# The diagonal term of a chunked attention from narrow products, and a shorter router, in a fused attention, router and MLP kernel

## The chip, the cores and the metric

The kernel runs on one core of one Trainium2 chip. Its time is the device time in microseconds (us) of one execution. Five engines work beside each other, each through its own queue of instructions: TensorE (PE, its weight loads PEld), VectorE (DVE), ScalarE (ACT), GpSimd (POOL) and SyncE (SP), which here only issues transfers. An instruction waits at the head of its engine's queue until what it reads is there and what it overwrites is free.

## The reference

Three parts follow each other: a linear attention with a state that decays per channel, a mixture of 8 experts with one expert per token, and a gated MLP.

```python
# attention: B, H, S, D = 4, 8, 768, 48
for t in range(S):
    cur = np.einsum('bhd,bhe->bhde', u[None] * kt, vt)
    y[:, :, t] = np.einsum('bhd,bhde->bhe', rt, state + cur)
    state = wt[:, :, :, None] * state + np.einsum('bhd,bhe->bhde', kt, vt)
# experts: N, D, E, F = 3072, 384, 8, 1024
logits = xn @ en.T / tau                  # x and expert_emb divided by (norm + 1e-6)
expert_idx = np.argmax(logits, axis=1)
probs = np.exp(logits - logits.max(-1, keepdims=True))
probs /= probs.sum(-1, keepdims=True) + 1e-09
out[mask] = gate_w[mask, None] * (np.maximum(x[mask] @ w1[e], 0.0) @ w2[e])
# second MLP: 384 -> 2048 -> 384
g = h * np.tanh(log1p(exp(h)))            # h = x @ w_in
return g @ w_out
```

The term `cur` is the bonus: for one token it adds (sum over d of r·u·k) times v. In a chunk of tokens it stands on the diagonal of the matrix of products of r and k.

## The kernel before

**Attention** (`attention`). The 768 tokens are cut into 12 chunks (NCH) of C = 64. Each chunk s holds 16 blocks (NB: 4 batches times 4 pairs of heads); on the 128 partitions lie the channels of two heads, 64 rows each (48 used). Per chunk, in `scaled`: ScalarE squares `w` for a check of its range (L513), VectorE scans `w` forwards (`pre`, L516), takes a reciprocal (L518) and scans backwards (`suf`, L520); GpSimd multiplies r by `pre` into `rh` and VectorE k by `suf` into `kh`, both in two halves of 128x512 (L525). In `scores`: ScalarE scales r by u into `ur` (4 instructions, L548); TensorE forms the dots of `kh` and `rh` (64 products of 64x64, L543) and, by the same helper `dots`, those of k and `ur`. The attention matrix `at` of a chunk has a half per head of the pair. For head 0 VectorE copies the dots under the mask `after` (strictly later tokens, L554); for head 1 ScalarE copies all of them (L556), and GpSimd clears what is not later by two selects (L558). Then VectorE copies, for both heads, the diagonal of the products of k and `ur` under the mask `same` (L563). In `carried`: TensorE transposes `kh` (L575), ScalarE copies that (L578), TensorE forms the sums for the state (L587), VectorE, or VectorE and GpSimd, the new state (L597, L600 and L602). In `outputs`: TensorE multiplies `rh` with the state (L616) and `at` with v (L621), and ScalarE copies the result to `x` (L631).

**Loads.** SyncE loads w, r, k and v of the chunks; each has two or three buffers (NW, NR, NK, NV = 3, 2, 3, 3; r and k as loaded have NR = 2), so a load waits for the last reader of the buffer's last contents. All loads stand in one queue (L487).

**Router** (`Router`). Every chunk gives two tiles of 128 tokens. `tile`: TensorE transposes the tile (L324), ScalarE copies it (L332) and sums its squares (L333), TensorE forms the logits (six half products, L329), ScalarE copies them (L335). `decide` runs over groups of tiles, ROUTED = [6, 6, 4, 4, 2, 2]: 20 small VectorE operations per group find the expert, its gate and the row (`inv_norm` L274 to L279, L356 to L360, ranks L378 to L382, gate L384 to L388), with matmuls for the running count (L369 to L373). `send` (L394) scatters each tile's rows to its experts' slots by a GpSimd transfer `xs`.

**Behind it** come short warming matmuls (L972), the experts (`experts`) and the second MLP (`moe2`). They start when the last send has been issued.

**The order.** All of attention and router is a list of steps, each with its engine, an estimated cost, what it reads and what it writes. `Plan.order` is a list scheduler: by the costs, the wake times and due times (`late`) it chooses the next step, and so fixes every engine's queue and which of the seven PSUM banks a step gets. A step is one or several instructions; `at`, `ur`, `kh` and so on name the tiles that the profile prints.

Of the kernel before, what the change touches and what calls it, by code (L numbers as in the profile page):

```python
# [43 lines left out]
ROUTED = [6, 6, 4, 4, 2, 2]  # L44
# [10 lines left out]
STEP, APART = 0.12, 0.0  # L55
FAR, LEAST = 45.0, 1e-10
LN_EXP = 6

# [10 lines left out]
class Plan:  # L69
# [13 lines left out]
    def add(self, eng, us, fn, reads=(), writes=(), wake=None, late=0.0, port=None, apart=0.0):  # L83
        o = SimpleNamespace(eng=eng, us=us, fn=fn, wake=self.WAKE[eng] if wake is None else wake, need=set(),
                            late=late, apart=apart, port=eng == "pool" if port is None else port, n=len(self.steps), ps=[k for k in {*reads, *writes} if k[0] == "ps"])
# [49 lines left out]
    def wait(self, o, q):  # L135

        return 0.0 if o.eng == q.eng and o.eng in ("pe", "sp") else o.wake

    def order(self):
        S = self.steps  # L140
        way = [0.0] * len(S)
        out = [[] for _ in S]
        for o in S:
            for p in o.need:
                out[p].append(o.n)
        for o in reversed(S):
            way[o.n] = o.us + max([self.wait(o, S[q]) + way[q] for q in out[o.n]] + [o.late])
        waits = [len(o.need) for o in S]
        ready = {o.n: 0.0 for o in S if not o.need}
        at, done = {}, {}  # L150
        banks = [(0.0, b) for b in self.g.banks]
        left = {k: len(u) for k, u in self.users.items()}
        seen = {}
        while ready:
            can = []
            for n, t in ready.items():
                o = S[n]
                t = max(t, at.get(o.eng, 0.0), at.get("port", 0.0) if o.port else 0.0, at.get("apart", 0.0) if o.apart else 0.0)
                new = sum(k not in self.bank for k in o.ps)
                if new:  # L160
                    if len(banks) < new:
                        continue
                    t = max(t, sorted(x[0] for x in banks)[new - 1])
                can.append((t, n))
            t0, n0 = min(can)
            eng = S[n0].eng
            first = lambda cs: min(cs, key=lambda c: (-way[c[1]], c[1]))
            t, n = first([c for c in can if S[c[1]].eng == eng and c[0] <= t0 + SLACK])
            if S[n].port:
                t, n = first([c for c in can if S[c[1]].port and c[0] <= t + SLACK])  # L170
                eng = S[n].eng
            o = S[n]
            for k in o.ps:
                if k not in self.bank:
                    banks.sort(key=lambda x: x[0])
                    self.bank[k] = banks.pop(0)[1]
            o.fn()
            del ready[n]
            at[eng] = t + o.us
            if o.port:  # L180
                at["port"] = t + o.us
            if o.apart:
                at["apart"] = t + o.apart
            done[n] = t + o.us
            for k in o.ps:
                left[k] -= 1
                seen[k] = max(seen.get(k, 0.0), t + o.us + o.wake)
                if not left[k]:
                    banks.append((seen[k], self.bank[k]))
            for q in out[n]:  # L190
                waits[q] -= 1
                if not waits[q]:
                    ready[q] = max(done[p] + self.wait(S[p], S[q]) for p in S[q].need)
        assert len(done) == len(S)


def dve(n):
    return 0.07 + n / 960


def act(n):
    return 0.06 + n / 1150
# [6 lines left out]
def setup(g, tmp, plan, then):  # L209
# [9 lines left out]
    g.oh, g.dest, g.desti = t("oh", [128, NT, E], BF16), t("dest", [128, NT]), t("desti", [128, NT], I32)  # L219
# [26 lines left out]
def setup_experts(g, tmp, plan, then):  # L246
# [9 lines left out]
    rn = inv_norm(g, plan, ss, *[tmp.tile([E, 1], F32, name=f"nrme{i}") for i in range(4)], "e", "e_ss", "e_rn")  # L256
# [9 lines left out]
def inv_norm(g, plan, ss, r, t, r2, out, nm, src, dst):  # L266
# [31 lines left out]
class Router:  # L298


    def __init__(self, g, pool, plan, sizes, xs):
# [7 lines left out]
            ("ss", [128, G]), ("lg", [128, G, E]), ("ca", [128, G, E]), ("nr", [128, G]), ("rn", [128, G]), ("sm", [128, G]))}) for i in range(2)]  # L309
        self.group = [(q, sum(sizes[:q]), n) for q, n in enumerate(sizes) for _ in range(n)]  # L310

    def tile(self, j):
# [18 lines left out]
        add("pe", 0.4, turn, [kx, "ident"], [k])  # L331
        add("act", 0.42, lambda: nc.scalar.copy(xT, plan.view(k, KC, 128)), [k], [kT])  # L332
        add("act", 0.7, lambda: nc.scalar.activation(self.sq, x[:, :DM], AF.Square, accum_out=q.ss[:, i:i + 1]), [kx], [("ss", par, i)])  # L333
        add("pe", 0.4, logits, [kT, "enT"], [k])
        add("act", 0.2, lambda: nc.scalar.copy(q.lg[:, i], lg()), [k], [("lg", par, i)])  # L335
# [3 lines left out]
    def decide(self, qi, j0, G):  # L339
# [3 lines left out]
        ss, sm, gt = q.ss[:, :G], q.sm[:, :G], self.xs[:, j0 % NX:j0 % NX + G, DM]  # L343
        at = iter(range(SMALL + 72 * par, 512, 6))
        mx, mn, nt, r2 = [g.bank[:, c:c + G] for c, _ in zip(at, range(4))]
        d = g.bank[:, SMALL + 72 * par + 24:][:, :G * E].rearrange("p (t e) -> p t e", e=E)
        one = lambda x: x.rearrange("p (t o) -> p t o", o=1).to_broadcast(full)
        lg, ca = q.lg[:, :G], q.ca[:, :G]
# [15 lines left out]
        rn = inv_norm(g, self.plan, ss, q.nr[:, :G], nt, r2, q.rn[:, :G], f"x{par}", ("ssall", par), kn)  # L364
# [3 lines left out]
        def rank():  # L368
            nc.tensor.matmul(rt()[:, :G].rearrange("p t e -> p (t e)"), lhsT=g.tri, rhs=oh.rearrange("p t e -> p (t e)"), start=True, stop=False)  # L369
            nc.tensor.matmul(rt()[:, G], lhsT=g.ones, rhs=oh[:, 0], start=False, stop=G == 1)  # L370
# [979 lines left out]
```

## Time and profile before

| | |
|---|---|
| runs of the kernel | 837.56 us (median of 832.56, 837.56, 838.58) |
| the execution profiled | 838.25 us; its span, from first to last instruction, 836.4 us |
| busy in the span | PE 770.5, DVE 651.7, ACT 487.5, POOL 401.9 us |
| TensorE's granted clock, mean | 0.960 |
| last send of the router issued | 187.24 us |
| attention and router, 0 to 187.24 us | PE 138.72, DVE 138.68, ACT 95.73, POOL 89.19 us busy |
| experts and second MLP, 199.00 to 836.40 us | PE 621.59 of 637.40 us busy |

The granted clock is a share of full speed. In a row of a view grouped by lines, the busy time is followed by the mean length of one instruction in ns and by the idle time of the engine just before these instructions, with what ended it. A mean can be longer than busy time divided by count, since instructions of one engine overlap.

### The profile page before, as it was taken

What the parts mean: (1) busy time and instruction counts of PE and PEld (TensorE: products, weight loads), DVE (VectorE), ACT (ScalarE), POOL (GpSimd) and SP (SyncE); (2) the same over time, 40 slices, a digit from 0 to 9 for tenths busy, and PEclk for the clock granted to TensorE, in tenths of its full rate; (3) what the DMA queues carried; (4) which work ended last, traced back from release to release, by engine and by line L of the source; (5) the groups of instructions that cost most, each with busy time, mean ns of one, the idle gap of its engine ahead of it and who ended that gap; (6) DMA issues with size and microseconds to landing.
All of it is one profiled execution on the core that took longest, in us unless ns stands there. A gap on an engine that the chain in (4) does not pass through costs nothing. (4 is left out here: it accounts for less than half of the span.)

```text
span 836.4 us, 18791 instructions
## 1 busy us (share of the span) xinstructions
PE 770.5 (92%) x7152; PEld 704.1 (84%) x7152; DVE 651.7 (78%) x999; ACT 487.5 (58%) x1000; POOL 401.9 (48%) x378
## 2 busy tenths in 40 slices
PE   2887788968999999999999999999999999999995
PEld 2776676747999999889989999999999999999995
DVE  9888867447889888998978887786876886877783
ACT  4664554424665566457556666656656656655653
POOL 7354454335677787776623344334334334334331
PEclk9898879869999999999999999999999999999998
DMA  6665445117777767767500000001001001001001
GB/s 166 175 183 165 148 140 160 54 74 185 185 201 200 181 188 196 192 153 215 127 1 1 1 10 29 1 1 39 1 0 38 1 1 38 0 1 38 1 1 42
DMA packets 61362, 73.87 MB, mean 88 GB/s; under 512 B 8966, under 2 KB 51886, under 8 KB 61262
## 3 DMA queue, kind: packets, MB, share of 16 engines
q1 hardware_dynamic: 57422, 63.11, 27.9%
q0 software_dynamic: 3840, 9.47, 3.1%
q8 instruction: 58, 0.95, 0.5%
q14 instruction: 42, 0.34, 0.1%
HBM read 61.86 MB, written 10.69 MB: 87 GB/s over the span
## 5 line engine op out<-in xcount | busy, mean ns | idle before, releaser
L1142 POOL TENSOR_TENSOR t<-t,t 128x512 f32<-128x512 f32 x94 | 122.0, 1299 | 237.2 <-ACT t L1138 234.4
L1151 DVE TENSOR_TENSOR gl<-t,gh 128x512 fp32r<-128x512 f32 (+1 forms) x97 | 114.1, 1176 | 74.5 <-ACT gh L1148 74.2
L1135 ACT ACTIVATE t<-t,two 128x512 f32<-128x512 f32 (+1 forms) x97 | 69.9, 720 | 118.4 <-DVE t L1132 118.4
L863 PE MATMUL acc<-woh,gl 128*128 128x384 f32 x384 | 129.6, 338 | 0.1
L861 PE MATMUL acc<-woh,gh 128*128 128x384 f32 x384 | 129.3, 337 | 0.0
L862 PE MATMUL acc<-wol,gh 128*128 128x384 f32 x384 | 129.0, 336 | 0.0
L940 POOL TENSOR_TENSOR w0l<-r,w0h 128x384 fp32r<-128x384 f32 x63 | 68.3, 1084 | 59.4 <-ACT w0h L939 53.1
L856 PE MATMUL ph<-xl,wih 128*128 128x512 f32 x240 | 95.0, 396 | 0.0
L855 PE MATMUL ph<-xh,wil 128*128 128x512 f32 x240 | 94.8, 395 | 0.0
L854 PE MATMUL ph<-xh,wih 128*128 128x512 f32 x240 | 93.3, 389 | 0.0
L861 PEld LDWEIGHTS acc<-woh,gh 128*128 128x128 f32 x384 | 72.2, 188 | 4.2
L862 PEld LDWEIGHTS acc<-wol,gh 128*128 128x128 f32 x384 | 72.1, 188 | 4.0
L940 POOL TENSOR_TENSOR w1l<-r,w1h 128x384 fp32r<-128x384 f32 x63 | 74.5, 1183 | 2.0 <-ACT w1h L939 1.5
L863 PEld LDWEIGHTS acc<-woh,gl 128*128 128x128 f32 x384 | 72.0, 188 | 0.4 <-DVE gl L1151 0.4
L856 PE MATMUL acc<-hl,w1h 128*128 128x428 f32 (+7 forms) x192 | 67.3, 350 | 3.8 <-DVE hl L1021 3.6
L1145 DVE TENSOR_TENSOR t<-t,ph 128x512 f32<-128x512 f32 (+1 forms) x97 | 64.8, 668 | 5.8 <-POOL t L1142 5.7
L854 PE MATMUL acc<-hh,w1h 128*128 128x428 f32 (+7 forms) x192 | 67.6, 352 | 1.8 <-DVE yT L1036 1.8
L1148 ACT CAST gh<-t 128x512 fp32r<-128x512 f32 (+1 forms) x97 | 58.8, 606 | 16.6 <-DVE t L1145 14.2
L1132 DVE SCALAR_TENSOR_TENSOR t<-t 128x512 f32<-128x512 f32 (+1 forms) x97 | 66.2, 683 | 2.1 <-ACT t L1128 2.1
L1125 DVE TENSOR_SCALAR t<-ph 128x512 f32<-128x512 f32 (+1 forms) x97 | 65.3, 674 | 2.1 <-PE ph L856 1.7
L855 PE MATMUL acc<-hh,w1l 128*128 128x428 f32 (+7 forms) x192 | 66.1, 344 | 0.0
L854 PE MATMUL ph<-xh,w0h 128*128 128x420 f32 (+7 forms) x189 | 65.0, 344 | 0.0
(213 smaller groups left out, 1810.6 us busy)
## 6 DMA issues: line engine op xcount, KB each, us to landing
r<-in_moe_w SPq DMA_DIRECT2D x128, 192.0 KB
d<-in_moe_w_in SPq DMA_DIRECT2D x16, 384.0 KB
d<-in_moe_w_out SPq DMA_DIRECT2D x16, 384.0 KB
r<-in_r_t SPq DMA_DIRECT2D x24, 192.0 KB
k<-in_k_t SPq DMA_DIRECT2D x24, 192.0 KB
v<-in_v_t SPq DMA_DIRECT2D x24, 192.0 KB
w<-in_w_t SPq DMA_DIRECT2D x22, 198.0 KB
xs<-zs SPq DMA_DIRECT2D x1, 1203.1 KB
```

What stands on the lines that cost most here:

```text
L854: mm(out, lhsT=wh, rhs=xh, start=start, stop=False)
L855: mm(out, lhsT=wl, rhs=xh, start=False, stop=False)
L856: mm(out, lhsT=wh, rhs=xl, start=False, stop=stop)
L861: mm(out, lhsT=ah, rhs=bh, start=start, stop=False)
L862: mm(out, lhsT=ah, rhs=bl, start=False, stop=False)
L863: mm(out, lhsT=al, rhs=bh, start=False, stop=stop)
L940: (eng or nc.gpsimd).tensor_tensor(lo, r, f32(hi), op=ALU.subtract)
L1125: nc.vector.tensor_scalar(tile_of(i, "t0", mt, bufs=3)[:, q], S[i]["ph"][:, q], 20.0, None, op0=ALU.min)
L1132: nc.vector.scalar_tensor_tensor(t0, t0, 2.0, t0, op0=ALU.add, op1=ALU.mult)
L1135: nc.scalar.activation(tile_of(i, "t1", mt)[:, q], S[i]["t0"][:, q], AF.Ln, bias=g.two)
L1142: (nc.gpsimd if i < TI - 2 else nc.vector).tensor_tensor(t0, t0, S[i]["t1"][:, q], op=ALU.mult)
L1151: nc.vector.tensor_tensor(tile_of(i, "gl", ghl, F32R)[:, q], S[i]["t0"][:, q], f32(S[i]["gh"][:, q]), op=ALU.subtract)
```

## The change

**The bonus.** Per chunk GpSimd multiplies r by k without scaling into one buffer `rk` (two halves, L551 of the new kernel). TensorE multiplies each 128x128 block of it by a narrow matrix `ub` of 2 columns, u of either head (8 products), with two filler products of 128x512 in bf16 ahead of them (FILL), and ScalarE copies the 128x16 results to `bon`. For head 0 ScalarE writes `same` scaled by a column of `bon` into `at` (8 instructions of 128x64), for head 1 GpSimd multiplies `same` by `bon` in one instruction of 128x512 (`ON_POOL`). The dots of `kh` and `rh` come after that, and VectorE copies them into `at` under `after`, for both heads. The scaling `ur`, the products of k and `ur`, ScalarE's copy, the selects and the copies under `same` are gone. The range check looks at `bon` too.

**The router** has five groups, [6, 6, 6, 4, 2]; the normalisation has one operation fewer; the running count is added by a matmul with the identity and kept by a ScalarE copy; 1e-9 stands as a ninth column that the sum takes in; the logits take three whole products.

**The order** is no longer computed. `ORDER` lists all steps in sequence and `BANKS` gives the PSUM banks, so each engine's queue follows the list.

```diff
-ROUTED = [6, 6, 4, 4, 2, 2]
+ROUTED = [6, 6, 6, 4, 2]
+FILL = 2
+ON_POOL = [(s, 1) for s in range(NCH)]
+ORDER = [
+    2, 16, 18, 6, 3, 4, 10, 0, 20, 19, 27, 9, 8, 11, 5, 7, 31, 12, 17, 32, 25, 29, 37, 38,
...
+]
...
     def order(self):
...
+        bank = iter(BANKS)
+        for n in ORDER:
+            o = self.steps[n]
             for k in o.ps:
                 if k not in self.bank:
+                    self.bank[k] = self.g.banks[int(next(bank))]
             o.fn()
...
-            ("dve", lambda: v.scalar_tensor_tensor(t, ss, -0.5, r, op0=ALU.mult, op1=ALU.mult), [src, kr], kt),
-            ("dve", lambda: v.tensor_tensor(t, t, r, op=ALU.mult), [kr], kt),
-            ("dve", lambda: v.scalar_tensor_tensor(r2, t, 1.5, r, op0=ALU.add, op1=ALU.mult), [kr], kt),
-            ("dve", lambda: v.tensor_tensor(t, ss, r2, op=ALU.mult), [src], kt),
-            ("dve", lambda: v.tensor_scalar(t, t, 1e-6, None, op0=ALU.add), [], kt),
+            ("dve", lambda: v.tensor_tensor(t, ss, r, op=ALU.mult), [src, kr], kt),
+            ("dve", lambda: v.tensor_tensor(r, t, r, op=ALU.mult), [kt], kr),
+            ("dve", lambda: v.scalar_tensor_tensor(t, r, -3.0, t, op0=ALU.add, op1=ALU.mult), [kr], kt),
+            ("dve", lambda: v.tensor_scalar(t, t, -0.5, 1e-6, op0=ALU.mult, op1=ALU.add), [], kt),
...
-                for h in COLS:
-                    nc.tensor.matmul(lg()[h], lhsT=xT[:, c, h], rhs=g.enT[:, c], start=c == 0, stop=c == KC - 1)
+                nc.tensor.matmul(lg(), lhsT=xT[:, c], rhs=g.enT[:, c], start=c == 0, stop=c == KC - 1)
...
+            nc.tensor.matmul(rt(), lhsT=g.ident, rhs=g.runs[:, qi:qi + 1].to_broadcast([128, G + 1, E]), start=False, stop=G == 1)
...
-        add("dve", n, lambda: v.tensor_tensor(rk(), rk(), g.runs[:, qi:qi + 1].to_broadcast(full), op=ALU.add), [("runs", qi), kr], [RK])
-        add("dve", n, lambda: v.tensor_tensor(g.runs[:, qi + 1], g.runs[:, qi], rt()[:, G], op=ALU.add), [kr, ("runs", qi)], [("runs", qi + 1)])
...
-        add("dve", n, lambda: v.tensor_scalar(sm, sm, 1e-9, None, op0=ALU.add), [], [SM])
...
-        for j in range(NP):
-            add("act", 0.43, lambda j=j: a.activation(UR[:, B * j:B * j + B], R[nr][:, B * j:B * j + B], AF.Copy, scale=uc[:, j:j + 1]),
-                [("r", nr), "uc"], [("ur", j)])
-        add("pe", 1.08, dots(ks, KH[nk], RH[nk]), hats, ks, late=late(s) + LATE_A)
-        add("dve", 0.63, lambda: v.copy_predicated(at[:, 0], mask(after), plan.view(ks[0], 2 * NP, C)),
-            [ks[0], "masks"], [("at", n, 0)])
-        add("act", act(512), lambda: a.copy(at[:, 1], plan.view(ks[1], 2 * NP, C)), [ks[1]], [("at", n, 1)])
-        for q in range(2):
-            add("pool", 0.65, lambda q=q: p.affine_select(
-                out=at[ROW[q], 1], in_=at[ROW[q], 1], pattern=[[0, 2 * NP], [1, C]], compare_op=ALU.is_ge, fill=0.0,
-                base=-1, channel_multiplier=-1), [], [("at", n, 1)])
-        add("pe", 1.08, dots(kb, K[nr], UR), [("k", nr)] + [("ur", j) for j in range(NP)], kb)
-        for h in range(2):
-            add("dve", 0.63, lambda h=h: v.copy_predicated(at[:, h], mask(same), plan.view(kb[h], 2 * NP, C)),
-                [kb[h], "masks"], [("at", n, h)])
+        def bonus():
+            for _ in range(FILL):
+                pe.matmul(plan.view(kb, 512), lhsT=g.ident.bitcast(BF16)[:, :128], rhs=g.wide, start=True, stop=True)
+            for jp in range(2 * NP):
+                pe.matmul(plan.view(kb, 2 * NP, 2)[:, jp], lhsT=RK[:, 2 * jp:2 * jp + 2].rearrange("p b t -> p (b t)"), rhs=ub[:, jp // 2],
+                          start=True, stop=True)
+
+        def own(h):
+            for jp in range(2 * NP):
+                a.activation(at[:, h, jp], same, AF.Copy, scale=BON[:, s, jp, h:h + 1])
+
+        for i, c in enumerate(halves):
+            add("pool", 1.2, lambda c=c: p.tensor_tensor(RK[:, c], R[nr][:, c], K[nr][:, c], op=ALU.mult),
+                [("r", nr), ("k", nr)], [("bon", i)])
+        add("pe", 0.9 + 0.22 * FILL, bonus, [("bon", 0), ("bon", 1), "ub", "ident", "wide"], [kb], recs=32 + 2 * FILL)
+        add("act", 0.2, lambda: a.copy(BON[:, s], plan.view(kb, 2 * NP, 2)), [kb], [("own b", s)])
+        for h in range(2):
+            if (s, h) in ON_POOL:
+                add("pool", 1.19, lambda h=h: p.tensor_tensor(at[:, h], same.rearrange("p (o t) -> p o t", o=1).to_broadcast([128, 2 * NP, C]),
+                                                              bc(BON[:, s, :, h]), op=ALU.mult), [("own b", s), "masks"], [("at", n, h)])
+            else:
+                add("act", 8 * 0.35, lambda h=h: own(h), [("own b", s), "masks"], [("at", n, h)])
+        add("pe", 1.08, dots, hats, ks, late=late(s) + LATE_A, recs=128)
+        for h in range(2):
+            add("dve", 0.71, lambda h=h: v.copy_predicated(at[:, h], mask, plan.view(ks[h], 2 * NP, C)), [ks[h], "masks"], [("at", n, h)])
```

How the queues move. First VectorE, in the middle of the chunks of the kernel before; the numbers behind the names are buffers (`pre_141`, `pre_142` are used in turn, and `at_117`, `at_118`):

```order
L600 TENSOR_TENSOR sum_126<-bank_80,state_125 128x384
L518 RECIPROCAL w_134<-pre_141 128x16
L563 COPY_PREDICATED at_117<-same_132,bank_83 128x512
L563 COPY_PREDICATED at_117<-same_132,bank_84 128x512
L520 SCALAR_TENSOR_TENSOR suf_143<-w_134,bank_79 128x1056
L554 COPY_PREDICATED at_118<-after_131,bank_81 128x512
L516 SCALAR_TENSOR_TENSOR pre_142<-w_135,bank_79 128x1056
L525 TENSOR_TENSOR kh_112<-k_138,suf_143 128x512 x2
```

And VectorE in the changed kernel, at a like place (L509 and L513 are now the scans, L511 the reciprocal, L518 `kh`, L565 the copy with `after`, L601 the sum):

```order
L518 TENSOR_TENSOR kh_109<-k_139,suf_144 128x512 x2
L509 SCALAR_TENSOR_TENSOR pre_141<-w_134,bank_79 128x1056
L565 COPY_PREDICATED at_115<-after_131,bank_85 128x512
L511 RECIPROCAL w_134<-pre_141 128x16
L565 COPY_PREDICATED at_115<-after_131,bank_80 128x512
L513 SCALAR_TENSOR_TENSOR suf_143<-w_134,bank_79 128x1056
L601 TENSOR_TENSOR sum_124<-bank_85,state_122 128x384
```

Three masked copies stood around the two scans of a chunk; now two stand there, both with `after`. GpSimd in the kernel before, at such a place:

```order
L525 TENSOR_TENSOR rh_115<-r_136,pre_141 128x512 x2
L558 AFFINE_SELECT at_118<-at_118 64x512 x2
L525 TENSOR_TENSOR rh_116<-r_137,pre_142 128x512
L602 TENSOR_TENSOR state_125<-sum_126,own_127 128x384 x2
L525 TENSOR_TENSOR rh_116<-r_137,pre_142 128x512
```

And GpSimd in the changed kernel (`rk` is L551, `rh` L518, the spread of head 1 L558, the state L603):

```order
L518 TENSOR_TENSOR rh_113<-r_136,pre_141 128x512 x2
L558 TENSOR_TENSOR at_115<-same_132,bon_129 128x512
L518 TENSOR_TENSOR rh_114<-r_137,pre_142 128x512
L551 TENSOR_TENSOR rk_140<-r_137,k_139 128x512 x2
L603 TENSOR_TENSOR state_122<-sum_124,own_125 128x384
L518 TENSOR_TENSOR rh_114<-r_137,pre_142 128x512
```

The two selects per chunk became one spread, and the two halves of `rk` stand in the queue ahead of the state and the second half of `rh`.

## Rows read from the trace of the kernel before

**Rows 1.** Busy time per stretch, with counts, granted clock, transfers' share.
```profile
core 0: us, PE busy (x) PEld busy (x) DVE busy (x) ACT busy (x) POOL busy (x), PEclk, DMA share, GB/s
57.21:130.83 73.62, 59.25 (x1687) 52.42 (x1679) 57.33 (x97) 42.99 (x119) 32.97 (x36) 0.84 0.50 156
...
0.00:187.24 187.24, 138.72 (x3849) 119.15 (x3850) 138.68 (x292) 95.73 (x261) 89.19 (x110) 0.85 0.47 140
199.00:836.40 637.40, 621.59 (x3245) 576.79 (x3243) 507.17 (x694) 386.78 (x728) 310.47 (x266) 1.00 0.26 71
```

**Rows 2.** By line, VectorE, 0 to 187.24: busy, mean ns, idle before, releaser.
```profile
L516 DVE TENSOR_TENSOR_SCAN pre<-w,bank 128x1056 f32<-128x1056 f32 x12 | 28.1, 2340 | 4.4 <-DMA w<-in_w_t 4.4
...
L563 DVE COPY_PREDICATED at<-same,bank 128x512 f32<-128x512 int32 x24 | 16.3, 714 | 9.1 <-ACT ur L548 5.5 <-PE bank L543 3.5
L525 DVE TENSOR_TENSOR kh<-k,suf 128x512 f32<-128x512 f32 x24 | 15.7, 689 | 1.0 <-DMA k<-in_k_t 1.0
L554 DVE COPY_PREDICATED at<-after,bank 128x512 f32<-128x512 int32 x12 | 8.6, 720 | 1.4 <-PE bank L543 1.4
...
L387 DVE TENSOR_SCALAR r_sm<-r_sm 128x6 f32<-128x6 f32 (+2 forms) x6 | 5.7, 944 | 0.0
...
L279 DVE RECIPROCAL r_rn<-bank 128x6 f32<-128x6 f32 (+2 forms) x6 | 1.1, 178 | 0.1
...
L658 DVE MEMSET at<- 128x512 f32 x2 | 1.0, 485 | 0.1
```

**Rows 3.** Timeline of VectorE and of GpSimd at 90 us: start, length.
```profile
90.36 3.87 DVE L387 TENSOR_SCALAR r_sm<-r_sm 128x6 f32<-128x6 f32 x1
...
90.30 1.62 POOL L602 TENSOR_TENSOR state<-sum,own 128x384 f32<-128x384 f32 x2
91.88 2.31 POOL L525 TENSOR_TENSOR rh<-r,pre 128x512 f32<-128x512 f32 x2
```

**Rows 4.** Waits of SyncE's queue, 0 to 187.24: total, times, longest.
```profile
SPq L487 <- PE bank L543: 27.3, 8, 11.5
```

**Rows 5.** By line, GpSimd, 0 to 187.24, columns as in rows 2.
```profile
L525 POOL TENSOR_TENSOR rh<-r,pre 128x512 f32<-128x512 f32 x24 | 28.6, 1205 | 25.8 <-DMA r<-in_r_t 18.4 <-DVE r_sm L386 6.1 <-DVE w L518 1.1
L394 POOL DMA_INDIRECT xs<-x,desti x24 | 24.1, 1006 | 30.0 <-DVE bank L357 10.0 <-issue 9.5 <-DVE kh L525 4.9
L558 POOL TENSOR_SCALAR_AFFINE_SELECT at<-at 64x512 f32<-64x512 f32 x24 | 15.7, 656 | 29.8 <-ACT at L556 20.4 <-DMA xs<-x,desti 8.7
```

**Rows 6.** Timeline of VectorE and of GpSimd at 80 us: start, length.
```profile
81.04 0.92 DVE L525 TENSOR_TENSOR kh<-k,suf 128x512 f32<-128x512 f32 x1
...
80.22 2.79 POOL L525 TENSOR_TENSOR rh<-r,pre 128x512 f32<-128x512 f32 x2
```

**Rows 7.** By line, ScalarE, 0 to 187.24, columns as in rows 2.
```profile
L548 ACT ACTIVATE ur<-r,uc 128x256 f32<-128x256 f32 x48 | 20.9, 501 | 7.7 <-PE bank L543 4.2 <-remote 3.4
...
L556 ACT COPY at<-bank 128x512 f32<-128x512 f32 x12 | 7.0, 585 | 14.6 <-PE bank L543 14.0 <-POOL rh L525 0.5
...
L385 ACT ACTIVATE r_lg<-r_lg 128x48 f32<-128x48 f32 (+2 forms) x6 | 1.4, 227 | 6.4 <-DVE r_lg L384 4.2 <-DVE f_ok L703 2.2
```

**Rows 8.** By line, TensorE, 0 to 187.24, columns as in rows 2.
```profile
L543 PE MATMUL bank<-ur,k 64*64 64x64 f32 x768 | 20.4, 243 | 8.2 <-issue 6.2 <-ACT ur L548 1.1 <-DVE at L554 0.9
...
L329 PE MATMUL bank<-enT,r_xT 128*64 128x8 f32 x288 | 14.7, 235 | 0.1
```

**Rows 9.** By line, TensorE, 182.8 to 192.6.
```profile
L972 PE MATMUL bank<-ident 128*128 128x256 bf16 x60 | 9.5, 339 | 0.0
```

**Rows 10.** Timeline of VectorE, 105 to 150: the twelfth scan forwards.
```profile
130.83 2.35 DVE L516 TENSOR_TENSOR_SCAN pre<-w,bank 128x1056 f32<-128x1056 f32 x1
```

**Rows 11.** Timeline of GpSimd, 184 to 212: the last send.
```profile
186.27 0.97 POOL L394 DMA_INDIRECT xs<-x,desti  x1 [0.30 <-issue]
```

**Rows 12.** Waits of TensorE, 0 to 187.24: total, times, longest.
```profile
PE bank L543 <- issue: 6.7, 12, 3.1
```

More of the change, by code (lines that the diff above doesn't have):

```diff
@@ L81, in __init__, with add @@
         self.g, self.steps, self.writer, self.readers, self.bank, self.users = g, [], {}, {}, {}, {}
-    def add(self, eng, us, fn, reads=(), writes=(), wake=None, late=0.0, port=None, apart=0.0):
-        o = SimpleNamespace(eng=eng, us=us, fn=fn, wake=self.WAKE[eng] if wake is None else wake, need=set(),
-                            late=late, apart=apart, port=eng == "pool" if port is None else port, n=len(self.steps), ps=[k for k in {*reads, *writes} if k[0] == "ps"])
+    def add(self, eng, us, fn, reads=(), writes=(), wake=None, late=0.0, port=None, apart=0.0, recs=0):
+        o = SimpleNamespace(eng=eng, us=us, recs=recs, fn=fn, wake=self.WAKE[eng] if wake is None else wake, need=set(),
+                            late=late, apart=apart, port=eng == "pool" if port is None else port, n=len(self.steps), ps=[k for k in dict.fromkeys([*reads, *writes]) if k[0] == "ps"])
         for k in reads:
@@ L133, in run @@
                     free.append(self.bank[k])
-    def wait(self, o, q):
-        return 0.0 if o.eng == q.eng and o.eng in ("pe", "sp") else o.wake
     def order(self):
[L140 to L172, printed above, removed]
@@ L173, in order @@
+        bank = iter(BANKS)
+        assert sorted(ORDER) == list(range(len(self.steps)))
+        for n in ORDER:
+            o = self.steps[n]
             for k in o.ps:
                 if k not in self.bank:
-                    banks.sort(key=lambda x: x[0])
-                    self.bank[k] = banks.pop(0)[1]
+                    self.bank[k] = self.g.banks[int(next(bank))]
             o.fn()
[L178 to L193, printed above, removed]
@@ L342, in decide @@
         v, q = nc.vector, self.q[par]
[L343 to L346, printed above, removed]
+        ss, gt = q.ss[:, :G], self.xs[:, j0 % NX:j0 % NX + G, DM]
+        at = iter(range(SMALL + 78 * par, 512, 6))
+        mx, mn, nt, sm, dest = [g.bank[:, c:c + G] for c, _ in zip(at, range(5))]
+        d = g.bank[:, SMALL + 78 * par + 30:][:, :G * E].rearrange("p (t e) -> p t e", e=E)
         one = lambda x: x.rearrange("p (t o) -> p t o", o=1).to_broadcast(full)
-        lg, ca = q.lg[:, :G], q.ca[:, :G]
+        lgs, lg, ca = q.lg[:, :G], q.lg[:, :G, :E], q.ca[:, :G]
         kr = ("ps", "rt", qi)
@@ L537, in scores @@
         hats = [(nm + "h", nk, i) for nm in "rk" for i in range(2)]
-        ks, kb = [[("ps", nm, s, h) for h in range(2)] for nm in "ab"]
-        def dots(k, x, y):
-            def fn():
-                for jp, h, q in blocks():
-                    pe.matmul(plan.view(k[h], 2 * NP, C)[ROW[q], jp], lhsT=x[ROW[h], 2 * jp + q], rhs=y[ROW[h], 2 * jp + q],
-                              start=True, stop=True)
-            return fn
-        for j in range(NP):
-            add("act", 0.43, lambda j=j: a.activation(UR[:, B * j:B * j + B], R[nr][:, B * j:B * j + B], AF.Copy, scale=uc[:, j:j + 1]),
-                [("r", nr), "uc"], [("ur", j)])
@@ L561, in scores, with dots @@
-        add("pe", 1.08, dots(kb, K[nr], UR), [("k", nr)] + [("ur", j) for j in range(NP)], kb)
-        for h in range(2):
-            add("dve", 0.63, lambda h=h: v.copy_predicated(at[:, h], mask(same), plan.view(kb[h], 2 * NP, C)),
-                [kb[h], "masks"], [("at", n, h)])
+        ks, kb = [("ps", "a", s, h) for h in range(2)], ("ps", "b", s)
+        at = AT[n]
+        def dots():
+            for jp, h, q in blocks():
+                pe.matmul(plan.view(ks[h], 2 * NP, C)[ROW[q], jp], lhsT=KH[nk][ROW[h], 2 * jp + q], rhs=RH[nk][ROW[h], 2 * jp + q],
+                          start=True, stop=True)
@@ L591, in carried @@
         more = s >= BUSY
-        add("pe", 2.4 if more else 1.08, sums, [("kb", n, 0), ("kb", n, 1), ("v", s % NV)] + [("state", n, q) for q in range(2) if more], ku)
+        add("pe", 2.4 if more else 1.08, sums, [("kb", n, 0), ("kb", n, 1), ("v", s % NV)] + [("state", n, q) for q in range(2) if more], ku, recs=136 if more else 128)
         for q in range(2):
@@ L656, in attention @@
         add("dve", 0.95, lambda n=n: v.memset(W[n], 1.0), [], [("w", n)])
-    for n in range(2):
-        add("dve", 0.48, lambda n=n: v.memset(AT[n][:, 0], 0.0), [], [("at", n, 0)])
+    add("dve", 0.06, lambda: v.memset(ub, 0.0), [], ["ub"])
+    for h in range(2):
+        add("dve", 0.1, lambda h=h: v.tensor_copy(ub[ROW[h], :, h], uc[ROW[h]]), ["uc"], ["ub"])
     for n in range(NV):
@@ L702, in within_range @@
     add("dve", 0.3, lambda: v.tensor_reduce(okm[:, 1:2], own, axis=AX.X, op=ALU.min), [("own", s) for s in range(NCH)], ["ok1"])
+    kbon = [("own b", s) for s in range(NCH)]
+    add("dve", 0.3, lambda: v.tensor_tensor(bon, bon, bon, op=ALU.mult), [], kbon)
+    add("dve", 0.3, lambda: v.tensor_scalar(bon, bon, HUGE, None, op0=ALU.is_le), [], kbon)
+    add("dve", 0.3, lambda: v.tensor_reduce(okb, bon, axis=AX.X, op=ALU.min), kbon, ["okb"])
+    add("dve", 0.15, lambda: v.tensor_tensor(okm[:, 1:2], okm[:, 1:2], okb, op=ALU.mult), ["okb"], ["ok1"])
     add("dve", 0.15, lambda: v.tensor_tensor(ok16, okm[:, 0:1].to_broadcast([128, 2]), okm[:, 1:2].to_broadcast([128, 2]), op=ALU.mult),
         ["ok0", "ok1"], ["ok16"])
-    add("pe", 0.1, lambda: nc.tensor.matmul(ps(), lhsT=g.ones, rhs=ok16, start=True, stop=True), ["ones", "ok16"], [k])
+    add("pe", 0.1, lambda: nc.tensor.matmul(ps(), lhsT=g.ones, rhs=ok16, start=True, stop=True), ["ones", "ok16"], [k], recs=2)
     add("dve", 0.15, lambda: v.tensor_scalar(g.flag[:, 0:1], ps()[:, 0:1], 127.5, None, op0=ALU.is_lt), [k], ["flag0"])
```

89 lines of the change are left out of this document (50 added, 39 removed), and 32 rows, old and new, of the table ORDER.

## Prediction

> **What bounds the kernel now.** I read the stretches first. Up to 187.24 us, where the last router row's send ends, the attention and the router fill the time; from 199.00 us on TensorE is busy for 621.59 of 637.40 us at a granted share of 1.00, the higher level of 2.4 GHz [rows 1]. The change touches nothing behind the last send, so the program is a stage of 187.24 us plus a fixed rest of 838.25 − 187.24 = 651.0 us, and what the stage loses or gains passes one to one. (The execution profiled took 838.25 us, 0.69 above the median of 837.56, within the runs' spread. The sum is made against 838.25.)
>
> In the stage no engine is full: TensorE 138.72, VectorE 138.68, ScalarE 95.73, GpSimd 89.19 us of 187.24, and in the middle stretch VectorE still has 57.33 of 73.62 [rows 1]. It is a chain of 12 chunks over four engines. Two readings decide what a cut is worth. VectorE carries the two scans per chunk, 2 × 28.1 us, and all that follows waits for them; they stand in VectorE's queue behind the masked copies, so any instruction taken out ahead of a scan brings it forward (the idle time in front of all `pre` scans is only 4.4 us) [rows 2]. And the `same` copies wait 9.1 us, 5.5 for the scaled r and 3.5 for the products: a link that the change cuts [rows 2].
>
> **Part 1, VectorE's instructions.** Out go 24 `same` copies (16.3 us); in come 12 more `after` copies, since h = 1 now takes them too: 24 × 0.68 becomes 12 × 0.72, a net −16.3 + 8.6 = −7.7 us; going by busy time per copy [rows 2]. The router has 16 instead of 20 small operations per group (normalisation one fewer, the 1e-9 addition and two run additions gone) and five groups for six, plus one copy of runs: 120 → 81; the embeddings' normalisation has one fewer, and five small ones are new in the setup: −35 × 0.178 (the small reciprocal of L279) = −6.2 us. Six of the removed, L387, took 5.7 us instead of 6 × 0.178 = 1.1, because one of them stood 3.87 us: −4.6 more [rows 2, 3]. Two 128x512 memsets go, −1.0 [rows 2]. Four operations in the range check are new, three of them on 192 columns, priced at twice the small one, the fourth as one: +1.2. Sum −7.7 − 6.2 − 4.6 − 1.0 + 1.2 = −18.3 us of VectorE work. Not all counts: VectorE is busy for 138.68 / 187.24 = 0.74 of the stage [rows 1], and an operation in a gap brings nothing. Between half (−9.2) and all (−18.3) I take 0.74: **−13.5**.
>
> **Part 2, the waits for the bonus.** The 9.0 us at the `same` copies (5.5 + 3.5) go, for the diagonal is now written ahead of the dots. Behind it the copies with `after` wait for the dots of both halves: 1.4 us for the 12 of now, so 1.4 more for the 12 new ones [rows 2]. Bounds −9.0 and 0 (the copy may simply wait as long for the diagonal). The order puts RK and the diagonal well ahead of the dots, so: **−7.6**.
>
> **Part 3, the loads.** SyncE's load queue waits 27.3 us for L543, the products that read k last [rows 4]. After the change the last reader of `k` is r·k on GpSimd, early in the chunk. What this is worth on the path is at most the 4.4 us that the scans wait for `w` [rows 2]; from 0 to −4.4, taken as **−3**.
>
> **Part 4, GpSimd and VectorE on the same data paths.** GpSimd gets 24 halves of r·k at 1.205 (28.9 us, priced as `rh`, the same form) and 12 spreads of the same size (14.5), and gives up 24 selects (15.7): +27.7, so 116.9 busy [rows 1, 5]. Its own time I take as hidden, price 0: it idles for 187.24 − 89.19 = 98 us now, of which 20.4 is waiting for ScalarE's copy that no longer exists [rows 5]; if that cover is gone, it is rival C. But its tensor operations disturb VectorE's. At 81.04 us a `kh` half ran against `rh` and took 0.92 instead of 0.69; GpSimd's pair took 2.79 where another took 2.31 [rows 2, 3, 6]. With more GpSimd operations on offer, each of 24 `kh` halves may meet one: 24 × 0.23 = **+5.5**. From below 0 (most halves meet none today), from above a wait for a whole GpSimd operation, 24 × 1.205 = +28.9.
>
> The Trainium skill, "SBUF — State Buffer", section "SBUF: two separate sides", says that VectorE and GpSimd share one port pair, an exclusive lock which an operation holds for its whole length while the other blocks; VectorE takes part with two SBUF inputs against a GpSimd operation that reads SBUF. The trace agrees that one waits for the other (2.79 against 2.31, 3.87 for a small operation), but at 81.04 shows 0.23 rather than 1.205 lost. By the rule the term would be +28.9 and the time 843 (rival B).
>
> **Part 5, ScalarE and TensorE.** ScalarE drops 48 scalings (20.9 us, 1.74 a chunk) and a copy of 0.585, together 2.33 a chunk; it gets a small copy, about 0.2 by the operation of 48 columns, and 8 scalings of 64 columns, each between 0.227 (48 columns) and 0.501 (256 columns) [rows 7]. At 0.25 that is 2.2, at 0.501 it is 4.2 a chunk, +22 us on an engine that idles for 91 us: 0, bounded by 0 and +22 × 0.51 = +11 (its busy share). TensorE drops 768 products of 20.4 us and gets per chunk 8 narrow ones (16 passes at 14.7 / 288 = 0.051) and two fillers of 512 columns, each at most twice the 0.339 of 256 columns: 0.82 + 1.36 = 2.2 against 1.7 [rows 8, 9]. They need r, k alone, so they stand in gaps; 0, within ±6 (12 × 0.5). The six half products of the router become three: hidden with them.
>
> **Sum:** −13.5 − 7.6 − 3 + 5.5 = −18.6, so 838.25 − 18.6 = **819.6 us**, with the last send starting near 186.27 − 18.6 = 167.7 and the twelfth `pre` scan near 130.83 − 14 = 117 (its share of parts 1 and 3) [rows 10, 11].
>
> **Rivals.**
> A, more is won. Everything taken from VectorE counts (−4.8 more), no half collides (−5.5), and half of the 6.7 us that TensorE spends starting L543 [rows 12] goes with 768 products (−3.4): 819.6 − 13.7 = 806. For it: the chain of chunks is tightest at VectorE. Against it: VectorE idles for 48 us now.
>
> B, one collision each. Every `kh` half waits for one GpSimd operation: 819.6 + 24 × (1.205 − 0.23) = 843. For it: the 3.87 us of L387 beside GpSimd's four operations [rows 3]. Against: 81.04 us [rows 6].
>
> C, GpSimd becomes the bound. 116.9 busy, plus 9.5 in which it waits for nothing that is shown at its sends [rows 5], plus 24 × 0.69 in which `kh` blocks it, is 143 of the 168.6 that the stage would have: 26 us are left for waits, of which it has 98 now. With half of those (49) the stage is 192 long and the time 843; with 35, 829. Middle: 838, no change.
>
> D, slower. VectorE starves behind GpSimd operations that stand back to back: in the changed order two `rk` or `rh` halves and a spread stand in a row. If a `kh` half waits for a pair (2.31), 819.6 + 24 × (2.31 − 0.23) = 869.5. It decides from 838.25 × 1.01 = 846.6 on, that is at 0.23 + 27.0 / 24 = 1.36 us lost per half. For it: L387, where a small operation stood while four GpSimd operations ran through [rows 3]. Against: among 24 `kh` halves (mean 0.689) no such wait stands now [rows 2].
>
> **How the numbers follow.** Forecast 0.48 (809 to 829.5: part 1 from half to all gives +4.3 and −4.8, part 2 to zero +7.6, the rest −5.5 and −1.4), A 0.18, B 0.07, C 0.15, D 0.12. One per cent, about what a measurement of this kernel can tell from no change, is 8.4 us. Faster by more: 0.48 + 0.18 + 0.02 of C = 0.68. Within: the rest of C and B, 0.20. Slower: D, 0.12. The range runs from 800 (A with a few us more) to 842 (into B and C); outside lie about 0.03 below and 0.16 above.
>
> **What the changed profile would show.** Right: last send starting at 165 to 171 us, twelfth scan at 114 to 120, VectorE busy for about 120 us in the stage, `kh` mean near 0.9, GpSimd 117, the eight small scalings near 0.25 each and no long wait at the copies with `after`. Wrong: `kh` mean above 1.4 or `rh` far above 1.205 (B or D); GpSimd busy or blocked almost throughout with VectorE waiting for `rh` products (C); ScalarE's eight scalings at 0.5, with TensorE waiting for them; TensorE's clock share in the stage, 0.85 now [rows 1], falling since it has less to do.

## The result and the profile after

The changed kernel takes 822.43 us (median of 20 runs, 818.8 to 832.66) beside 833.38 us for the kernel before (20 runs on the same chip): a ratio of 0.9874, interval 0.9854 to 0.9893, or about 10.5 us less. Ratios and intervals, here and below, leave out the executions that took over 1.5 per cent more than the fastest of the same kernel; the medians take in all (one execution, of the run with the doubled copies, took 4247.46 us). By the ratio the change is faster by a little more than one per cent, and the time lies inside the range of the prediction (800 to 842, forecast 819.6). The execution profiled took 821.62 us, near its median; the one of before, 838.25 us, on which the sum was made, lay 4.9 us above the median that 20 runs give. So the two profiles differ by 16.6 us, the kernels by 10.5.

The stretches of the changed kernel, columns as in [rows 1]; the last send now ends at 169.82 us:

```profile
0.00:169.82 169.82, 146.59 (x3169) 131.26 (x3170) 124.90 (x247) 92.80 (x310) 118.86 (x123) 0.92 0.52 155
0.00:57.21 57.21, 43.51 (x976) 39.50 (x978) 51.15 (x72) 35.01 (x103) 48.15 (x58) 1.00 0.67 189
57.21:115.00 57.79, 54.30 (x1199) 50.04 (x1197) 42.99 (x66) 31.55 (x113) 39.74 (x37) 0.88 0.56 169
115.00:155.00 40.00, 38.21 (x955) 33.17 (x947) 24.25 (x59) 23.06 (x82) 21.79 (x20) 1.00 0.29 93
```

The stage is 17.4 us shorter, the rest of the program 821.62 − 169.82 = 651.8 against 651.0: it was untouched, as taken. VectorE lost 13.8 us of work (138.68 to 124.90). TensorE gained 7.9, in a shorter stage: the bonus and the logits take 18.3 more (the lines below), all other lines together 10.4 less (103.6 to 93.2). It is now busy for 94 and 96 per cent of the two later stretches, 57 to 115 and 115 to 155 us. GpSimd is at 118.86 (116.9 were forecast). TensorE's granted clock in the stage rose from 0.85 to 0.92 of the upper level.

VectorE's lines in 0 to 169.82 us, columns as in [rows 2]:

```profile
L509 DVE TENSOR_TENSOR_SCAN pre<-w,bank 128x1056 f32<-128x1056 f32 x12 | 28.0, 2340 | 0.6 <-DMA w<-in_w_t 0.2 <-POOL rh L518 0.2
...
L518 DVE TENSOR_TENSOR kh<-k,suf 128x512 f32<-128x512 f32 x24 | 19.9, 849 | 0.1
L565 DVE COPY_PREDICATED at<-after,bank 128x512 f32<-128x512 int32 x24 | 16.5, 722 | 17.3 <-PE bank L536 17.2
```

The scans hardly wait any more (0.6 us, 4.4 before). But the copies under `after` wait 17.3 us for the dots (L536), where `same` and `after` together waited 10.5. The wait was not removed, it moved and grew. TensorE's lines show what stands in its queue:

```profile
L543 PE MATMUL bank<-ub,rk 128*128 128x2 f32 x192 | 25.5, 264 | 0.7 <-POOL rk L551 0.7
...
L321 PE MATMUL bank<-enT,r_xT 128*128 128x8 f32 x144 | 19.8, 262 | 0.9 <-ACT r_xT L324 0.9
L536 PE MATMUL bank<-rh,kh 64*64 64x64 f32 x768 | 17.6, 244 | 2.0 <-issue 1.7 <-ACT enT L255 0.3
...
L541 PE MATMUL bank<-wide,ident 128*128 128x512 bf16 x24 | 8.1, 421 | 0.0
```

The narrow products take 25.5 us, 0.133 each, not 0.051; with the fillers the bonus costs 33.6 us of TensorE instead of 20.4 [rows 8], and the three whole logit products 19.8 us instead of the 14.7 of six halves. All of it stands in the one queue from which the dots come, and TensorE itself idles only 2.0 us before the dots, so it is mostly the queue that VectorE waits for. SyncE's wait for L543, 27.3 us before, is 1.5. But r·k is not the last reader of `k`, as the prediction had it: `kh`, VectorE's product, reads `k` too and comes later, and SyncE now waits 13.6 us for it. In all, its load queue waits 51 us instead of 68.

```profile
SPq L480 <- DVE kh L518: 13.6, 4, 7.9
...
SPq L480 <- PE bank L543: 1.5, 3, 0.6
```

ScalarE's and GpSimd's new lines in the same stage, first the eight scalings and then `rk` and the spread of head 1:

```profile
L548 ACT ACTIVATE at<-same,bon 128x64 f32<-128x64 f32 x96 | 24.2, 339 | 0.2
...
L551 POOL TENSOR_TENSOR rk<-r,k 128x512 f32<-128x512 f32 x24 | 30.4, 1280 | 2.6 <-DMA v<-in_v_t 1.3 <-PE bank L317 1.1
...
L558 POOL TENSOR_TENSOR at<-same,bon 128x512 f32<-128x512 f32 x12 | 12.7, 1056 | 12.5 <-ACT bon L554 12.5
```

And the worst meeting of VectorE and GpSimd, the timelines of both at 90 us: one `kh` half stood while GpSimd's pair of `rh` ran through.

```profile
91.63 2.98 DVE L518 TENSOR_TENSOR kh<-k,suf 128x512 f32<-128x512 f32 x1
...
91.74 2.32 POOL L518 TENSOR_TENSOR rh<-r,pre 128x512 f32<-128x512 f32 x2
```

In another meeting, at 37 us, it was GpSimd that stood: two `kh` halves took 0.63 each, and one `rh` took 2.52, where the median `rh` takes 1.19.

```profile
37.80 1.27 DVE L518 TENSOR_TENSOR kh<-k,suf 128x512 f32<-128x512 f32 x2
...
37.60 2.52 POOL L518 TENSOR_TENSOR rh<-r,pre 128x512 f32<-128x512 f32 x1
```

### The profile page after: what moved, and what is told of

Its sections match the earlier page's. It is cut to its first block, busy times and chain, and to the rows that moved or that the text cites. A ratio compares the mean times of both kernels' runs of the same rounds, so it can differ in the third digit from the quotient of the medians.

```text
span 819.9 us, 17379 instructions
## 1 busy us (share of the span) xinstructions
PE 777.7 (95%) x6464; PEld 715.9 (87%) x6464; DVE 638.3 (78%) x954; ACT 484.6 (59%) x1049; POOL 431.7 (53%) x391
```

## The experiments

Three theories were held against each other at first. V: VectorE's chain still bounds, and TensorE's extra work stands in its gaps. T: TensorE's queue has become the bound of the middle of the stage. K: the fillers pay by holding TensorE's clock up. A fourth came with the first results: the operations bring nothing, the order of the table does. The ratios below are to the kernel before on the same chip. The chips differ (its median was 833.4, 820.6, 818.8 and 831.9 us in the four sets of runs), so times are compared on one chip only. Even the ratio of the changed kernel is not the same on two chips (0.9874 and, below, 0.9946), which weakens every comparison of ratios across chips.

**TensorE's work, more and less.** Fillers none, and six:

```diff
-FILL = 2
+FILL = 0      # first run
+FILL = 6      # second run
```

> The changed kernel without the two filler products per chunk (24 of 128x512, 8.1 us busy in the changed kernel's profile). Theory T (TensorE's queue has become the bound of the middle of the stage, busy 54.3 of 57.8 and 38.2 of 40.0 us): their time leaves the path, 4 to 8 us less than the changed kernel, about 815 to 818. Theory V (VectorE's chain still bounds, TensorE's narrow work stands in its gaps): within 2 us of the changed kernel, 822. Theory K (the fillers hold TensorE's clock up, 0.92 granted in the stage against 0.85 before): the clock of the stage falls towards 0.85 and the kernel is 3 to 10 us slower, 825 to 832.

> The changed kernel with six filler products per chunk instead of two: 48 more of 128x512, at 0.34 us busy each 16 us more on TensorE. T: nearly all of it on the path where TensorE is full, 8 to 16 us slower than the changed kernel, 830 to 838. V: hidden, 0 to 3 us. K: the clock rises a little further and pays part of it, 0 to 8 us.

Measured 813.41 us, ratio 0.9925 (0.9889 to 0.9961), and 824.52 us, 1.0042 (1.0005 to 1.008). The 72 products between the two are 72 × 8.1 / 24 = 24 us of TensorE's time; the ratios differ by 0.0117, 9.6 us (5 to 14 by the two intervals). So a microsecond of TensorE's work costs some 0.4 us (0.2 to 0.6), neither nothing (V) nor all (T). Theory K falls: without fillers the kernel is faster than with six, and its stage has 0.91 granted, with fillers 0.92 in the first profile of the changed kernel and 0.90 in the later one. The row is that of the run without fillers:

```profile
0.00:162.34 162.34, 142.10 (x3153) 130.79 (x3154) 124.61 (x247) 92.83 (x310) 117.75 (x123) 0.91 0.55 162
```

Weights of 64 columns instead of 128, for the logits, and for the bonus:

```diff
-                nc.tensor.matmul(lg(), lhsT=xT[:, c], rhs=g.enT[:, c], start=c == 0, stop=c == KC - 1)
+                for h in COLS:
+                    nc.tensor.matmul(lg()[h], lhsT=xT[:, c, h], rhs=g.enT[:, c], start=c == 0, stop=c == KC - 1)
```

```diff
-                pe.matmul(plan.view(kb, 2 * NP, 2)[:, jp], lhsT=RK[:, 2 * jp:2 * jp + 2].rearrange("p b t -> p (b t)"), rhs=ub[:, jp // 2],
-                          start=True, stop=True)
+                for q in range(2):
+                    pe.matmul(plan.view(kb, 2 * NP, 2)[ROW[q], jp], lhsT=RK[:, 2 * jp + q], rhs=ub[:, jp // 2], start=True, stop=True)
```

> The changed kernel with the router's logits as before in six products of 64 columns of weights per tile instead of three of 128 (19.8 us busy now, 14.7 before). T: 5 us less TensorE, 3 to 5 us faster, about 818. V: no difference (within 2 us). K: no difference, or slower by what the clock loses.

> The changed kernel with the bonus in 16 products with 64 columns of weights per chunk instead of 8 with 128 (now 25.5 us busy in 192 records, 0.133 each; if 64 columns cost 0.051 as the logits before, 384 records take 19.6). T: 3 to 6 us faster, 816 to 819. V: no difference. K: no difference.

Measured 814.93 us, ratio 0.9932 (0.9896 to 0.9967), and 816.83 us, 0.9967 (0.993 to 1.0004). Without the changed kernel on that chip these two decide nothing on the time. What they settle is the price: the line of the bonus on TensorE, in the run with 64 columns, has twice the records and 15.3 us instead of 25.5.

```profile
L544 PE MATMUL bank<-ub,rk 128*64 128x2 f32 x384 | 15.3, 207 | 3.9 <-POOL rk L551 3.0 <-issue 0.2
```

The weight loads of these products, in the changed kernel and then in that run (columns as in [rows 2]; PEld is TensorE's loading of weights), take as long as the line itself: 26.4 us of loading beside 25.5, and 14.0 beside 15.3. So a product with two columns to stream costs its weights. A single load is not much shorter with 64 columns (mean 151 ns, 215 with 128); but 384 of them lie in 14.0 us, so about four run beside each other, where it is under two in the changed kernel.

```profile
L543 PEld LDWEIGHTS bank<-ub,rk 128*128 128x128 f32 x192 | 26.4, 215 | 3.7 <-POOL rk L551 2.2
```

```profile
L544 PEld LDWEIGHTS bank<-ub,rk 128*64 128x64 f32 x384 | 14.0, 151 | 9.4 <-POOL rk L551 5.3 <-issue 3.2 <-POOL rh L518 0.4
```

Then on one chip: the changed kernel unaltered, both halves together, and both halves with no fillers (the edits are those above).

> The changed kernel once more, unaltered, as the yardstick for the other runs of this call on the same chip. On the first chip it stood at 0.9874 of the kernel before. All theories: 0.985 to 0.990.

> The changed kernel with both the bonus products (16 of 64 weight columns, which took 15.3 us of TensorE in the run of that edit alone, instead of 25.5) and the logits (six of 64, 12.5 instead of 19.8) in halves: 17 us less work on TensorE. T (TensorE's queue bounds the middle of the stage): at least half of it on the path, 7 to 14 us faster than the changed kernel. V (VectorE's chain bounds): within 3 us of it.

> Both halves and no fillers: 17 + 8 = 25 us less work on TensorE. T: 10 to 18 us faster than the changed kernel. V: within 3 us. K (TensorE's clock is held by the fillers): the clock of the stage falls and the kernel is slower than the same with fillers by 3 to 8 us.

Measured 814.79, 811.79 and 810.27 us; ratios 0.9946 (0.9910 to 0.9982), 0.9883 (0.9817 to 0.9949) and 0.9903 (0.9868 to 0.9938). On this chip the change is worth 0.5 per cent, less than on the first. TensorE's work in the stage went from 149.18 to 132.10 and 126.53 us, the ratio by 0.0063 and 0.0043, which is 5.2 and 3.5 us (3.0 and 4.5 by the medians): a share of 0.15 to 0.3, with intervals that overlap. T expected 7 to 14 and 10 to 18 us, V at most 3. The measured times lie between, nearer to V, and T's 10 us for the last run lies beyond its interval. The versions with halves have the lowest times, but their lead over the changed kernel is not beyond doubt.

What these cuts do shorten is the wait of VectorE's copies for the dots. It is 17.3 and 20.2 us in the two profiles of the changed kernel, 14.4 without fillers, 9.4 with the bonus in halves, and 7.8 with both halves and no fillers, so TensorE's work made a large part of it:

```profile
L566 DVE COPY_PREDICATED at<-after,bank 128x512 f32<-128x512 int32 x24 | 16.4, 721 | 7.8 <-PE bank L537 7.6
```

**VectorE's work, more.** Every copy under `after` made twice, which leaves the result as it is:

```diff
+            def masked(h=h):
+                for _ in range(2):
+                    v.copy_predicated(at[:, h], mask, plan.view(ks[h], 2 * NP, C))
-            add("dve", 0.71, lambda h=h: v.copy_predicated(at[:, h], mask, plan.view(ks[h], 2 * NP, C)), [ks[h], "masks"], [("at", n, h)])
+            add("dve", 0.71, masked, [ks[h], "masks"], [("at", n, h)])
```

> The changed kernel with every copy under the mask made twice: 24 more copies of 128x512, 24 x 0.72 = 17 us more work on VectorE, nothing on TensorE. V (an operation of VectorE counts by its busy share, 0.74, as the prediction took it): 12 us or 1.5 per cent slower than the changed kernel, so 1.002 to 1.010 of the kernel before. T (TensorE bounds the middle, VectorE waits 17 us for the dots anyway): 0 to 5 us, 0.987 to 1.000.

Measured 828.87 us, ratio 0.9965 (0.9933 to 0.9998). Its stage and its copies (0 to 177.46 us):

```profile
0.00:177.46 177.46, 150.14 (x3178) 134.59 (x3179) 143.89 (x271) 93.25 (x311) 117.85 (x123) 0.90 0.51 148
```

```profile
L567 DVE COPY_PREDICATED at<-after,bank 128x512 f32<-128x512 int32 x48 | 34.1, 728 | 11.7 <-PE bank L536 9.0 <-POOL rh L518 1.7
```

VectorE is busy for 19.0 us more than in the first profile of the changed kernel, and 0.9965 − 0.9874 = 0.009 is 7.6 us: a share of 0.4. Against the ratio of the other chip it would be 0.002, a share of 0.1, and the intervals run from nothing to 0.6. All of this is below the 0.74 of V, whose 1.002 to 1.010 was missed; T's 0.987 to 1.000 was met. Part of the added work vanished in the wait for the dots, 11.7 us now instead of 17.3, so the price holds for work at this place of the queue. Of the 19.0 us, 2.8 are in the `kh` halves, one of which stood through five GpSimd operations in a row (a pair of `rh`, a spread, a pair of `rk`):

```profile
95.83 6.14 DVE L518 TENSOR_TENSOR kh<-k,suf 128x512 f32<-128x512 f32 x1
```

So neither engine bounds alone: a microsecond of either was worth some 0.1 to 0.4, with intervals from nothing to 0.6, which fits a chain in which both wait for each other.

**The order.** The changed kernel with every operation as it is, but in the order, and with the choice of PSUM banks, that the list scheduler of the kernel before gives:

```diff
     def order(self):
-        bank = iter(BANKS)
-        for n in ORDER:
+        S = self.steps
+        way = [0.0] * len(S)
...
```

> The changed kernel with all its operations, but in the order that the list scheduler of the kernel before makes of them from the changed costs, in place of the table. If the gain comes from the operations, within 4 us of the changed kernel. If it comes from the table: most of the 11 us are lost, or the kernel is slower than before, since TensorE has 18 us more work (25.5 + 8.1 + 19.8 against 20.4 + 14.7).

Measured 831.54 us, ratio 1.0161 (1.0103 to 1.0218), on the same chip as the changed kernel's 814.79. The same operations are 16.7 us apart through their order (banks included), and without the table the change is slower than before. The profiles differ by less, 10.7 us, since the execution profiled of the changed kernel lay high (821.08). Three stretches of the changed kernel on that chip, the last its stage:

```profile
0.00:57.21 57.21, 42.73 (x886) 38.70 (x886) 48.34 (x67) 32.29 (x94) 45.19 (x55) 0.97 0.68 181
130.00:171.00 41.00, 37.55 (x722) 32.64 (x721) 21.95 (x93) 19.42 (x75) 22.05 (x21) 0.83 0.31 109
...
0.00:170.11 170.11, 149.18 (x3168) 133.30 (x3169) 123.84 (x247) 93.14 (x310) 118.16 (x123) 0.90 0.53 155
```

and of the list scheduler's order:

```profile
0.00:57.21 57.21, 37.50 (x726) 33.17 (x726) 44.84 (x55) 27.94 (x84) 42.21 (x53) 0.85 0.64 165
130.00:171.00 41.00, 40.60 (x913) 35.68 (x913) 18.01 (x56) 20.22 (x71) 17.80 (x18) 0.87 0.32 98
...
0.00:180.01 180.01, 152.03 (x3170) 136.83 (x3171) 129.91 (x247) 94.43 (x310) 117.83 (x123) 0.85 0.51 146
```

Every engine does less in the first 57 us (TensorE 5.2 us less, VectorE 3.5), and from 130 us on TensorE is full for 41 us (40.60 busy, 37.55 with the table). Its granted clock in the stage is lower too, 0.85 against 0.90, but TensorE is busy for only 2.9 us more, so by an estimate from these busy times a slower TensorE makes at most that much of the difference. The VectorE lines say where the list's order waits:

```profile
L559 DVE TENSOR_TENSOR_SCAN pre<-w,bank 128x1056 f32<-128x1056 f32 x12 | 28.1, 2344 | 8.8 <-DMA w<-in_w_t 5.8 <-issue 2.9
...
L615 DVE COPY_PREDICATED at<-after,bank 128x512 f32<-128x512 int32 x24 | 16.4, 725 | 7.4 <-PE bank L586 7.4
...
L648 DVE TENSOR_TENSOR state<-bank,own 128x384 f32<-128x384 f32 x8 | 4.1, 546 | 15.7 <-PE bank L638 15.7
```

The scans wait 8.8 us, 5.8 of it for `w` (0.9 and 0.6 with the table), the state 15.7 us for the sums (2.3 with the table). The copies under `after` wait less, 7.4 us instead of 20.2.

Three runs split that further, all ordered by the list scheduler: with TensorE's work cut (halves, no fillers); the new router with the old attention; the new bonus with the old router. The edits are whole functions taken from one kernel into the other.

> The list scheduler's order, as in the run before that stood at 1.016, with bonus products and logits in halves and no fillers: 25 us less TensorE. T: 8 to 16 us faster than with whole products, 0.996 to 1.006 of the kernel before. V: still about 1.012 to 1.016. If the table alone makes the gain, it stays above 1.000.

> The short router in five groups with the attention of the kernel before, ordered by the list scheduler: 39 small operations fewer on VectorE, 5 us more TensorE for the logits. V: 4 to 8 us faster than before, 0.990 to 0.995. T: 0 to 4 us slower, 1.000 to 1.005. If the scheduler finds a bad place for the larger groups: up to 1.01.

> The new bonus with the router of the kernel before in its six groups, ordered by the list scheduler: 12 masked copies fewer on VectorE, 13 us more on TensorE, 27 us more on GpSimd. V: faster, 0.985 to 0.995. T: 5 to 12 us slower than before, 1.006 to 1.015, since nothing but the order is then left to make the changed kernel's gain.

Measured ratios 1.0122 (1.0085 to 1.0159), 1.0092 (1.0057 to 1.0126) and 1.0110 (1.007 to 1.015). Taking the halves and fillers out of TensorE's work (143.09 us busy in the stage, 152.03 with them) does not heal the list's order: T's 0.996 to 1.006 is missed, so TensorE's added work alone was not what made it slow. The short router alone is slower than before, where V expected 0.990 to 0.995 and T 1.000 to 1.005. VectorE has 8.8 us less to do, but TensorE 12.0 more, 10.2 of them in the whole logit products (24.9 us instead of 14.7). Its stage is 191.51 us.

```profile
0.00:191.51 191.51, 150.75 (x3710) 132.98 (x3711) 129.91 (x254) 95.38 (x262) 88.46 (x110) 0.85 0.47 137
```

And so is the bonus alone, as T expected. VectorE is at 138.05, hardly less than before, since its `kh` halves take 21.9 us instead of 15.7; the stage is 188.63:

```profile
0.00:188.63 188.63, 150.38 (x3297) 132.16 (x3298) 138.05 (x285) 94.97 (x309) 118.03 (x123) 0.84 0.49 139
```

Two limits: the scheduler's constants are those set for the kernel before (the costs of the steps are the changed ones but for the last two runs, where the part taken from the kernel before keeps its old costs), and a scheduler tuned anew, or the old operations in a table of their own, was not tried. So what is shown is that these operations need another order than this list's to gain; how much a table would have given the old operations stays open.

## Why the prediction was right, and where not

**The frame** held. The rest is 650.1 to 652.3 us in all profiles, so everything happens in the stage. The last send starts at 168.84 us (forecast 167.7), the twelfth scan at 117.65 (117). Measured against the profile, −16.6 us stand beside −18.6. Against the 20 runs of each kernel it is −10.5: the profile of before was of an execution that lay high, which the three times shown did not tell.

**Part 1** had its work right and its worth too high. VectorE's busy time fell by 13.8 us (−18.3 and +5.5 of collisions were forecast, −12.8), but by the run with the copies made twice a microsecond counted not 0.74 but about 0.4, or 0.1 by the ratio of the other chip. At 0.4 that makes about −5.5 of the change in work instead of −13.5 + 5.5 = −8. That is carried over from copies added at one place; no run takes only VectorE's operations out.

**Part 2** failed. −7.6 was forecast; the wait of VectorE at the masked copies went from 10.5 to 17.3 us. The step took it that with the diagonal written ahead of the dots, 12 more copies would wait only 1.4 us more. But the dots come when TensorE's queue gets to them, with the narrow products and the fillers in that queue, and the wait fell to 7.8 us when that work was cut. A row of before pointed there: ScalarE's copy of the dots of head 1, which VectorE's new copies replace, waited 14.0 us for them [rows 7], and the step did not count it.

**Part 3** was right in size: −3 forecast, the scans' wait fell by 3.8. Its reason holds in part only: `kh`, not r·k, reads `k` last. And it belongs to the order: with the list scheduler the changed operations wait 8.8 us there, so the earlier release of `k` alone does not bring it.

**Part 4** came out near in size. The `kh` halves took 4.2 us more (15.7 to 19.9; +5.5 forecast), mean 0.849; but in the later profile of the same kernel they took 17.1, so the nearness is in part luck. That GpSimd's own work stayed hidden is read from the 51 us of the stage in which it still idles; no run tests it. Rivals B and D did not come about: one half met a pair and took 2.98, but the mean loss of a half is 0.16 us, where B needed 1.205 and D 1.36. What D describes did happen to the single half of 6.14 us in the run with the doubled copies. By the rule of the Trainium skill ("SBUF — State Buffer", "SBUF: two separate sides"), of a VectorE operation with two SBUF inputs and a GpSimd operation that reads SBUF, one holds the shared ports for its whole length and the other blocks; the trace agrees that a meeting blocks outright (2.98 beside 2.32, and on GpSimd's side 2.52 instead of 1.19). The 0.23 us of the meeting at 81 us were VectorE's side alone: GpSimd's pair lost 2.79 − 2.31 = 0.48 there, and the two make 0.71, about the length of a half [rows 6]. But only some ten of the 24 halves lie beside a GpSimd operation, in part it is GpSimd that stands, and the median half stayed at 0.679:

```profile
L518 DVE TENSOR_TENSOR kh<-k,suf x24: 626/679/2983, 10.0 to 142.7; 128x512 f32<-128x512 f32 x24
```

(VectorE's `kh` in the changed kernel: shortest, median and longest in ns.) C did not come about either: GpSimd is not busy or blocked throughout.

**Part 5** failed for TensorE. A narrow product was priced by the logits of before, whose weights have 64 columns; with 128 columns it takes 0.133 instead of 0.051. The bonus came to +13.2 us and the logits to +5.1 where ±6 was allowed, and the queue is nearly full from 57 to 155 us. At the 0.15 to 0.4 us that a microsecond of it cost in the runs, the 18 us gave back some 3 to 7, an estimate. ScalarE's scalings took 0.339, between the two bounds; whether they stayed hidden is not tested.

**What was not in the sum at all** is the order. It was costed at nothing and only read for what stands ahead of what. On the chip where both were run, the changed operations are 1.6 per cent slower than the kernel before in the list's order and 0.5 per cent faster in the table's: 2.1 per cent by the order, more than the whole change is worth there (0.5) or on the first chip (1.3). The forecast came out near because a gain left out (the order, some −17 us against this list) and losses left out (TensorE's 18 us, the wait for the dots) stood against each other; that the number fell into the range is luck as far as parts 1, 2 and 5 go. These items do not add up one by one to the measured −10.5, and how much of the order's gain belongs to these operations alone stays open. Of the reasons given, the frame is borne out, and parts 3 and 4 in their size. That fewer operations on VectorE would by themselves make the kernel faster is not shown: with the list's order it was slower, but no run took them away without adding work elsewhere.

## What to carry to other kernels

When a change replaces a scheduler's order by a fixed one, cost the order as a part of its own, by how early each engine fills up and what piles up at the end; under an order made for other operations a change can turn into a loss, as here. A narrow matmul was priced here by its weights, so take its price from a row with as many weight columns. In this chain without a full engine a microsecond of work was worth well under its engine's busy share, so look for the row of the wait that the work would shorten, on every engine whose work moves. And a profiled execution should be placed in the spread of the runs before a sum is made on it.

## What the runs showed that was not expected

The kernel before takes 818.8 to 833.4 us, in the median, in the four sets of runs, and the change is worth 1.3 per cent in one and 0.5 in another, with intervals that do not overlap. The granted clock of the stage is 0.90 to 0.95 in all kernels with the table and 0.83 to 0.85 in all with the list's order, whether the fillers are there (0.92 and 0.90) or not (0.91): it goes with the order, and which is the cause of which the runs do not tell.
